# First A^T W products started matrix by matrix, and the last chunk worked in two token halves

## Chip, cores and metric

One core of one Trainium2 chip. The metric is the device time of one execution in microseconds, as the median of several. At this core count a run counts as slow when it lies more than 1.5% above the fastest of its kernel.

## The reference, cut to what matters

```python
# q, k, v: (4, 6144, 256); w1, w2, w3: (256, 768); w_out: (768, 256); fp32 in and out
qn = q / (norm(q, axis=1) + 1e-6)
kn = k / (norm(k, axis=1) + 1e-6)
s = kn.transpose(0, 2, 1) @ qn / tau             # 256 x 256 for each of 4 batches
a = softmax(s)                                   # rows sum to 1
x = (v @ a).reshape(24576, 256)
h = maximum(maximum(x @ w1, x @ w2), x @ w3)
out = h @ w_out
```

The kernel never builds `x`. It multiplies A^T into each W once per batch (`aw`), so that `h = max over m of v @ aw[m]`.

## The kernel before

PE is the matrix engine (PEld in the profile is its weight loads), ACT the scalar, DVE the vector and POOL the GpSimd engine; SP only sends transfers here. PSUM is the memory that PE writes its products to, and to evict is to copy them out of it. Work runs in 48 chunks of 512 tokens. PE forms three h products for each of six column blocks (`h_block`); ACT copies the first out of PSUM, and DVE takes two maxima with the other two. The output products of a chunk (`o_steps`) stand between the h blocks of the next. PSUM has six buffers for h and other products (`ps_h`) and two more (`ps_x`). The parts that the change touches:

```python
def rowsums(et):                       # 1/sum of the exponentials, by four tiny matmuls
    rs_ps = htile("rs_ps")
    ...PE.matmul(rs_ps[:, ic:ic + 1], lhsT=et[:, j, ic * P:(ic + 1) * P], rhs=ones_c, ...)
    DVE.reciprocal(out=rinv, in_=rs_ps[:, 0:CC])

def aw_part(et, rinv, aw, fp, w):      # 12 products, 6 evictions, ACT and DVE in turn
    for m in range(3):
        for ic in range(CC):
            ew = htile("ew_ps")
            for j in range(CC):
                PE.matmul(ew[:, :w], lhsT=et[:, j, ic * P:(ic + 1) * P], rhs=w_sb[m][:, j, fsl], ...)
            ...  # ACT.activation or DVE.tensor_scalar_mul into aw[m], times rinv

def v_transpose_pe(gi):                # 8 PE transposes of the first chunk's v, then
    ...
    ACT.activation(out=vt[:, :half, :], in_=ps[:, :half, :], func=AF.Copy)
    DVE.tensor_copy(out=vt[:, half:, :], in_=ps[:, half:, :])

def h_block(gi, aw, fc):
    for m in range(3):
        t = htile(f"h_ps{m}")
        for ic in range(CC):
            PE.matmul(t, lhsT=aw[m][:, ic, fsl], rhs=vt[:, :, ic, :], ...)   # 512 columns
        hp.append(t)
    ACT.activation(out=s_mx, in_=hp[0], func=AF.Copy)
    DVE.tensor_tensor(out=s_mx, in0=hp[1], in1=s_mx, op=ALU.max)
    DVE.tensor_tensor(out=ht[:, fc, :], in0=hp[2], in1=s_mx, op=ALU.max)

def o_last(gi):                        # the last chunk's output products, all at the end
    pss = [xtile("o_ps") for _ in range(TPC // 2)]
    ...  # 24 matmuls of 256 columns
    ACT.activation(out=o0, in_=pss[0], func=AF.Copy)      # 512 columns each
    DVE.tensor_copy(out=o1, in_=pss[1])
    ACT.dma_start(out=dst[:, 0:2, :], in_=o_sb[:, 0:2, :])
    SP.dma_start(out=dst[:, 2:4, :], in_=o_sb[:, 2:4, :])

ps = gram(0)
...  # 8 warm-up matmuls
et = softmax_t(*ps)
aw = alloc_aw()
rinv = rowsums(et)
v_transpose_pe(0)
aw_part(et, rinv, aw, 0, FT)
```

Of the kernel before, what the change touches and what calls it, by code (L numbers as in the profile page):

```python
# [10 lines left out]
FP32 = mybir.dt.float32  # L11
BF16 = mybir.dt.bfloat16
FP8 = mybir.dt.float8e4
AF = mybir.ActivationFunctionType
ALU = mybir.AluOpType
# [16 lines left out]
def kernel(  # L32
# [13 lines left out]
    PE = nc.tensor  # L46
    DVE = nc.vector
    ACT = nc.scalar
    POOL = nc.gpsimd
    SP = nc.sync  # L50

    B, N, C = q.shape
    d_ff = moe_w1.shape[1]
    d_model = C
    P = 128
    CC = C // P
    FC = d_ff // P
    CHUNK = 512
    TPC = CHUNK // P
    NG = N // P  # L60
    NCH = N // CHUNK
# [14 lines left out]
    sm = ctx.enter_context(tc.tile_pool(name="sm", bufs=2))  # L76
# [8 lines left out]
    def htile(name):  # L85
        return ps_h.tile([P, 512], FP32, tag="h", name=name)

    def xtile(name, cols=512, dtype=FP32):
        return ps_x.tile([P, cols], dtype, tag="x", name=name)
# [159 lines left out]
    def softmax_t(ps, rkb):  # L249
        n2q = sm.tile([P, CC], FP32, name="n2q")  # L250
        scr = sm.tile([P, P], FP32, name="scr")
        for j in range(CC):
            DVE.tensor_tensor_reduce(out=scr, in0=ps[j][:, C:C + P], in1=ident, scale=1.0, scalar=0.0,  # L253
                                     op0=ALU.mult, op1=ALU.add, accum_out=n2q[:, j:j + 1])
        lnq = sm.tile([P, CC], FP32, name="lnq")
        rq = sm.tile([P, CC], FP32, name="rq")
        ACT.activation(out=lnq, in_=n2q, func=AF.Ln)
        ACT.activation(out=rq, in_=lnq, func=AF.Exp, scale=-0.5, bias=neg_ln_tau)
        return exp_t([ps[j][:, 0:C] for j in range(CC)], rkb, rq)


    def alloc_aw():
        return [aw_pool.tile([P, CC, d_ff], BF16, name=f"aw{m}_sb", tag=f"aw{m}") for m in range(3)]

    def rowsums(et):
        rinv = sm.tile([P, CC], FP32, name="rinv")
# [3 lines that stand above are left out]
                PE.matmul(rs_ps[:, ic:ic + 1], lhsT=et[:, j, ic * P:(ic + 1) * P], rhs=ones_c,  # L270
                          start=(ic == 0 and j == 0), stop=(j == CC - 1), skip_group_check=True)
        DVE.reciprocal(out=rinv, in_=rs_ps[:, 0:CC])
        return rinv

    def aw_part(et, rinv, aw, fp, w):
        fsl = slice(fp * w, (fp + 1) * w)
        n = 0
# [4 lines that stand above are left out]
                    PE.matmul(ew[:, :w], lhsT=et[:, j, ic * P:(ic + 1) * P], rhs=w_sb[m][:, j, fsl],  # L282
                              start=(j == 0), stop=(j == CC - 1))
                if n % 2 == 0:
                    ACT.activation(out=aw[m][:, ic, fsl], in_=ew[:, :w], func=AF.Copy,  # L285
                                   scale=rinv[:, ic:ic + 1])
                else:
                    DVE.tensor_scalar_mul(out=aw[m][:, ic, fsl], in0=ew[:, :w],  # L288
                                          scalar1=rinv[:, ic:ic + 1])
                n += 1  # L290


    vts = {}
    hts = {}
# [12 lines left out]
    def v_transpose_pe(gi):  # L307
        v_sb = v_tiles.pop(gi).rearrange("p t c -> p (t c)")
        vt = vt_tile(gi)
        vt_ps = xtile("vt_ps", cols=TPC * C, dtype=BF16)  # L310
        for i in range(TPC * CC):
            PE.matmul(vt_ps[:, i * P:(i + 1) * P], lhsT=v_sb[:, i * P:(i + 1) * P], rhs=ident,
                      is_transpose=True, start=(i == 0), stop=(i == CC * TPC - 1))
        half = TPC * CC // 2
        ps = vt_ps.rearrange("p (i n) -> p i n", n=P)
        ACT.activation(out=vt[:, :half, :], in_=ps[:, :half, :], func=AF.Copy)
        DVE.tensor_copy(out=vt[:, half:, :], in_=ps[:, half:, :])

    def h_block(gi, aw, fc):
        vt = vts[gi]  # L320
        ht = hts[gi]
        fsl = slice(fc * P, (fc + 1) * P)
        hp = []
        for m in range(3):
            t = htile(f"h_ps{m}")
            for ic in range(CC):
                PE.matmul(t.rearrange("p (t n) -> p t n", t=TPC), lhsT=aw[m][:, ic, fsl], rhs=vt[:, :, ic, :], start=(ic == 0), stop=(ic == CC - 1))  # L327
            hp.append(t)
        s_mx = mx_pool.tile([P, CHUNK], BF16, name="s_mx")
        ACT.activation(out=s_mx, in_=hp[0], func=AF.Copy)  # L330
        DVE.tensor_tensor(out=s_mx, in0=hp[1], in1=s_mx, op=ALU.max)  # L331
        DVE.tensor_tensor(out=ht[:, fc, :], in0=hp[2], in1=s_mx, op=ALU.max)  # L332

    def o_steps(gi):

# [18 lines left out]

        return [lambda t=t: step(t) for t in range(TPC)]

    def o_last(gi):

        ht = hts[gi]
        o_sb = o_pool.tile([P, TPC, d_model], FP32, name="o_sb")  # L360
        pss = [xtile("o_ps") for _ in range(TPC // 2)]
        for fcs in (range(FC - 1), (FC - 1,)):
            for t in range(TPC):
                half = slice((t % 2) * d_model, (t % 2 + 1) * d_model)
                for fc in fcs:
                    PE.matmul(pss[t // 2][:, half], lhsT=ht[:, fc, t * P:(t + 1) * P], rhs=wo_sb[:, fc, :],  # L366
                              start=(fc == 0 and t % 2 == 0), stop=(fc == FC - 1), skip_group_check=True)
        dst = out_r[gi // NCH, gi % NCH]
        o0 = o_sb[:, 0:2, :].rearrange("p t d -> p (t d)")
        o1 = o_sb[:, 2:4, :].rearrange("p t d -> p (t d)")  # L370
        ACT.activation(out=o0, in_=pss[0], func=AF.Copy)
        DVE.tensor_copy(out=o1, in_=pss[1])  # L372
        ACT.dma_start(out=dst[:, 0:2, :], in_=o_sb[:, 0:2, :])
        SP.dma_start(out=dst[:, 2:4, :], in_=o_sb[:, 2:4, :])


    ps = gram(0)
    warm_ps = htile("warm_ps")
    for i in range(8):
        PE.matmul(warm_ps, lhsT=ident, rhs=warm, start=(i == 0), stop=(i == 7))  # L380
    et = softmax_t(*ps)
    aw = alloc_aw()
    rinv = rowsums(et)
    v_transpose_pe(0)
    aw_part(et, rinv, aw, 0, FT)
    v_transpose(1)

    guard = consts.tile([P, 1], BF16, name="guard")
# [10 lines left out]
    for b in range(B):  # L399
        more = b + 1 < B  # L400
        if more:
            alloc_qk(b + 1)
        for ch in range(NCH):
            gi = b * NCH + ch
            hts[gi] = ht_pool.tile([P, FC, CHUNK], BF16, name="ht_sb")
            load_v(gi + 4)
            v_transpose(gi + 2)
            if gi == 1:
                hold_loads(2)
            if more and 1 <= ch < 9:  # L410
                load_k(b + 1, (ch - 1) * 6, 6)
                load_q(b + 1, (ch - 1) * 6, 6)
            gaps = [[] for _ in range(FC)]
            if ch == 0:
                if b == 0:
                    for fp in range(1, d_ff // FT):
                        gaps[2 * fp - 2].append(lambda fp=fp: aw_part(et, rinv, aw, fp, FT))
                else:
                    gaps[0].append(lambda: aw_part(et, rinv, aw, 1, FH))
            for s, f in enumerate(pending):  # L420
                gaps[s + 1].append(f)
            if more and 3 <= ch < 11:
                g0 = (ch - 3) * 6
                for i, (which, g) in enumerate(((1, g0), (1, g0 + SQW), (0, g0), (0, g0 + SQW))):
                    gaps[(0, 2, 3, 5)[i]].append(lambda which=which, g=g: square_piece(b + 1, which, g))
            if more and ch == 10:
                gaps[5].append(lambda: fold(b + 1))
            if more and ch == NCH - 1:
                st = {}
                gaps[0].append(lambda: st.update(n=norms(b + 1)))  # L430
                gaps[1].append(lambda: st.update(e=exp_t(gs, *st["n"])))
                gaps[4].append(lambda: st.update(r=rowsums(st["e"])))
            for fc in range(FC):
                h_block(gi, aw, fc)
                for f in gaps[fc]:
                    f()
            pending = o_steps(gi)
            if more and ch == NCH - 2:
                gs = gram_kq(b + 1)
            if more and ch == NCH - 1:  # L440
                et, rinv = st["e"], st["r"]
                aw = alloc_aw()
                aw_part(et, rinv, aw, 0, FH)
    o_last(B * NCH - 1)
    keep_order(tc)


# [33 lines left out]
```

## Time and profile before

| | before |
|---|---|
| median of 3 runs | 576.62 us (576.47 to 576.75) |
| span of the profiled run | 574.9 us |
| PE / DVE / ACT busy | 97% / 71% / 53% |
| PE without a hole from | 39.78 us |
| last PE work, last eviction, span end | 570.43, 571.15, 574.9 us |

Lines of the chain of waits read "start us, length us, what" and are a path back from the last instruction; lines of the timeline read "start us, us, engine, line, operation, out<-in, count, [idle before <- what ended it]". The line numbers of the two kernels differ: h products are L327 before and L360 after, the second maximum L332 and L366.

### The profile page before, as it was taken

How to read it: one execution, taken by the hardware profiler on the slowest of the kernel's cores; microseconds unless marked ns; L12 is line 12 of the kernel's file. 1: busy time of each engine (PE TensorE's matmuls, PEld its weight loads, DVE VectorE, ACT ScalarE, POOL GpSimd, SP SyncE). 2: the span in 40 equal slices, each digit the busy share in tenths (PEclk: the TensorE clock that was granted, in tenths of full speed). 3: DMA queues.
4: the chain of work that ended last, by engine and by line, in shares of the span. 5: the costliest groups of instructions: out<-in, count | busy, mean ns of one | idle time of the engine just before them, and what ended most of it. 6: DMA issues, size and time to landing. Idle time of an engine off the chain costs nothing.

```text
span 574.9 us, 9325 instructions
## 1 busy us (share of the span) xinstructions
PE 555.1 (97%) x3328; PEld 328.5 (57%) x3328; DVE 406.4 (71%) x627; ACT 307.2 (53%) x530; POOL 227.3 (40%) x235
## 2 busy tenths in 40 slices
PE   3789999999999999999999999999999999999996
PEld 3655555555755555555575555555575555555554
DVE  0048777777577777777748777777848778778774
ACT  1034567677454466776735447767646444444442
POOL 4232257776731028777761006777760000000000
PEclk9999999999999999999999999999999999999999
DMA  9998998885598228977378526788535234322111
GB/s 142 107 144 157 130 178 124 157 133 113 102 118 164 59 66 155 133 152 130 75 131 130 114 75 101 157 131 130 125 84 127 66 82 129 74 91 76 56 73 74
DMA packets 75951, 65.62 MB, mean 114 GB/s; under 512 B 52353, under 2 KB 61953, under 8 KB 75905
## 3 DMA queue, kind: packets, MB, share of 16 engines
q0 software_dynamic: 18928, 26.48, 39.1%
q1 hardware_dynamic: 56832, 38.28, 22.9%
q8 instruction: 26, 0.43, 0.3%
q10 hardware_dynamic: 144, 0.26, 0.1%
q14 instruction: 21, 0.16, 0.1%
HBM read 78.64 MB, written 25.17 MB: 181 GB/s over the span
## 4 chain that ended last, share of the span: by engine, by line
PE 93%; DMA 5%; ACT 0%; DVE 0%; issue 0%; POOL 0%; DVEq 0%; POOLq 0%
PE h_ps L327 65%; PE o_ps L346 21%; DMA q_sb<-in_q_dram 4%; PE gram L235 3%; PE ew_ps L282 3%; DMA k_sb<-in_k_dram 2%; PE o_ps L366 0%; PE gram L178 0%; PE n_ps L216 0%; PE n_ps L218 0%; ACT et L246 0%; PE gram L180 0%; DVE o_sb L372 0%; POOL k_sb L99 0%; DVE scr L253 0%
## 5 line engine op out<-in xcount | busy, mean ns | idle before, releaser
L327 PE MATMUL h_ps<-vt_sb,aw_sb 128*128 128x512 bf16 x1728 | 406.6, 379 | 0.0
L331 DVE TENSOR_TENSOR s_mx<-h_ps,s_mx 128x512 bf16<-128x512 f32 x288 | 197.9, 687 | 98.1 <-ACT s_mx L330 97.1
L327 PEld LDWEIGHTS <-aw_sb 128*128 128x128 bf16 x1728 | 168.2, 98 | 163.0 <-DVE aw_sb L288 3.7
L330 ACT ACTIVATE s_mx<-h_ps 128x512 bf16<-128x512 f32 x288 | 171.4, 595 | 130.7 <-PE h_ps L327 130.7
L332 DVE TENSOR_TENSOR ht_sb<-h_ps,s_mx 128x512 bf16<-128x512 f32 x288 | 199.2, 692 | 30.7 <-PE o_ps L346 0.5
L204 POOL TENSOR_TENSOR acc<-acc,sq 128x768 f32<-128x768 f32 x90 | 147.7, 1651 | 70.7 <-ACT sq L198 70.5
L346 PE MATMUL o_ps<-wo_sb,ht_sb 128*128 128x256 bf16 x1128 | 153.9, 273 | 0.0
L346 PEld LDWEIGHTS <-ht_sb 128*128 128x128 bf16 x1128 | 110.4, 98 | 52.9
L349 ACT ACTIVATE o_sb<-o_ps 128x512 f32<-128x512 f32 x94 | 56.1, 597 | 83.1 <-PE o_ps L346 83.1
L110 POOL DMA_DIRECT2D v_sb<-in_v_dram x48 | 26.8, 562 | 88.5 <-DMA vt_sb<-v_sb 86.6
L198 ACT ACTIVATE sq<-q_sb 128x768 bf16<-128x768 fp8e4 x48 | 40.5, 844 | 0.0
L198 ACT ACTIVATE sq<-k_sb 128x768 bf16<-128x768 fp8e4 x48 | 40.1, 835 | 0.0
L201 POOL CAST acc<-sq 128x768 f32<-128x768 bf16 x6 | 4.9, 821 | 64.6 <-ACT sq L198 64.6
L102 POOL DMA_DIRECT2D q_sb<-in_q_dram x32 | 17.7, 555 | 10.7 <-DMA k_sb<-in_k_dram 9.7
L166 PE MATMUL kk<-k_sb 128*128 128x256 fp8e4 x48 | 7.8, 339 | 11.7 <-DVE k_sb L152 5.4
L285 ACT ACTIVATE aw_sb<-ew_ps,rinv 128x384 bf16<-128x384 f32 (+1 forms) x27 | 14.4, 546 | 5.7 <-PE ew_ps L282 4.8
L282 PE MATMUL ew_ps<-w_sb,et 128*128 128x384 bf16 (+1 forms) x108 | 17.1, 308 | 0.0
L235 PE MATMUL gram<-k_sb,q_sb 128*128 128x512 fp8e4 x144 | 16.8, 277 | 0.0
L99 POOL DMA_DIRECT2D k_sb<-in_k_dram x29 | 16.0, 554 | 1.0 <-POOLq L462 0.8
L235 PEld LDWEIGHTS <-q_sb 128*128 128x256 fp8e4 x144 | 15.9, 136 | 0.6
L178 PE MATMUL gram<-k_sb,q_sb 128*128 128x512 fp8e4 x48 | 10.7, 323 | 3.4 <-DMA q_sb<-in_q_dram 3.4
L166 PEld LDWEIGHTS <-k_sb 128*128 128x256 fp8e4 x48 | 6.5, 182 | 12.8 <-DMA k_sb<-in_k_dram 6.3
(52 smaller groups left out, 103.6 us busy)
## 6 DMA issues: line engine op xcount, KB each, us to landing
out_dram<-o_sb SPq DMA_DIRECT2D x47, 512.0 KB, 2.8
v_sb<-in_v_dram POOLq DMA_DIRECT2D x48, 256.0 KB, 3.7
k_sb<-in_k_dram POOLq DMA_DIRECT2D x24, 192.0 KB, 5.3
q_sb<-in_q_dram POOLq DMA_DIRECT2D x24, 192.0 KB, 6.8
k_sb<-in_k_dram POOLq DMA_DIRECT2D x5, 256.0 KB, 10.8
q_sb<-in_q_dram POOLq DMA_DIRECT2D x5, 256.0 KB, 19.4
w_sb<-in_moe_w_dram POOLq DMA_DIRECT2D x9, 128.0 KB, 5.7
kf<-in_k_dram SPq DMA_DIRECT2D x2, 512.0 KB, 4.3
```

The costliest lines, as they stand in the source:

```text
L102: POOL.dma_start(out=qk[b][0][:, g0:g0 + w, :], in_=q_r[b][:, g0:g0 + w, :])
L110: POOL.dma_start(out=t, in_=v_r[gi // NCH, gi % NCH])
L198: ACT.activation(out=sq, in_=src, func=AF.Square)
L204: POOL.tensor_tensor(out=acc, in0=acc, in1=sq, op=ALU.add)
L235: PE.matmul(g[:, j * C:(j + 1) * C], lhsT=qt[:, tsl, j * P:(j + 1) * P], rhs=kt[:, tsl, :], start=(tp == 0 and j == 0), stop=(tp == NG // ...
L282: PE.matmul(ew[:, :w], lhsT=et[:, j, ic * P:(ic + 1) * P], rhs=w_sb[m][:, j, fsl], start=(j == 0), stop=(j == CC - 1))
L327: PE.matmul(t.rearrange("p (t n) -> p t n", t=TPC), lhsT=aw[m][:, ic, fsl], rhs=vt[:, :, ic, :], start=(ic == 0), stop=(ic == CC - 1))
L330: ACT.activation(out=s_mx, in_=hp[0], func=AF.Copy)
L331: DVE.tensor_tensor(out=s_mx, in0=hp[1], in1=s_mx, op=ALU.max)
L332: DVE.tensor_tensor(out=ht[:, fc, :], in0=hp[2], in1=s_mx, op=ALU.max)
L346: PE.matmul(st["ps"][:, half], lhsT=ht[:, fc, t * P:(t + 1) * P], rhs=wo_sb[:, fc, :], start=(fc == 0), stop=(fc == FC - 1))
L349: ACT.activation(out=st["o"][:, t - 1:t + 1, :].rearrange("p t d -> p (t d)"), in_=st["ps"], func=AF.Copy)
```

## The change

Its intent: in the head, fill PE's wait for the exponentials with the transposes and with the products whose weights have landed, and let DVE copy v first; in the tail, have half of the last chunk's output evicted and sent before the end. Cut to its core:

```diff
+    def aw_first(et, aw):
+        ...
+        products(0, (0, 1))          # first half of et, matrices 0 and 1
+        sums(0)
+        sums(1)
+        DVE.reciprocal(out=rinv, in_=rs_ps[:, 0:CC])
+        products(1, (0, 1))
+        for j in range(CC):
+            products(j, (2,))
+        ...                          # the same six evictions
@@ v_transpose_pe
+        DVE.tensor_copy(out=vt[:, half:, :], in_=ps[:, half:, :])
         ACT.activation(out=vt[:, :half, :], in_=ps[:, :half, :], func=AF.Copy)
-        DVE.tensor_copy(out=vt[:, half:, :], in_=ps[:, half:, :])
@@ h_block takes a token slice, so its matmuls, copy and maxima can be 256 columns wide
-    def o_last(gi):
+    def last_chunk(gi, aw, pending):
+        ...
+        for fc in range(FC):
+            h_block(gi, aw, fc, slice(0, HT))
+            if 1 <= fc <= len(pending):
+                pending[fc - 1]()             # output products of the chunk before
+        for fc in range(FC):
+            h_block(gi, aw, fc, slice(HT, TPC))
+            if fc >= FC - HT:
+                first_half(fc - (FC - HT))    # 6 output products; the 2nd call evicts and sends
+        ...                                   # 12 products of the second half, in two banks
+        ACT.activation(out=o_sb[:, HT, :], in_=pss[0][:, 0:d_model], func=AF.Copy)
+        DVE.tensor_copy(out=o_sb[:, HT + 1, :], in_=pss[1][:, 0:d_model])
+        ACT.dma_start(out=dst[:, HT, :], in_=o_sb[:, HT, :])
+        SP.dma_start(out=dst[:, HT + 1, :], in_=o_sb[:, HT + 1, :])
@@ head
-    for i in range(8):               # warm-up matmuls
+    for i in range(6):
     et = softmax_t(*ps)
+    v_transpose_pe(0)
     aw = alloc_aw()
-    rinv = rowsums(et)
-    v_transpose_pe(0)
-    aw_part(et, rinv, aw, 0, FT)
+    rinv = aw_first(et, aw)
```

More of the change, by code (lines that the diff above doesn't have):

```diff
@@ L290, in aw_part, with sums, products @@
                 n += 1
+    def aw_first(et, aw):
+        rinv = sm.tile([P, CC], FP32, name="rinv")
+        rs_ps = xtile("rs_ps")
+        parts = [(m, ic, htile("ew_ps")) for m in range(3) for ic in range(CC)]
+        def sums(j):
+            for ic in range(CC):
+                PE.matmul(rs_ps[:, ic:ic + 1], lhsT=et[:, j, ic * P:(ic + 1) * P], rhs=ones_c,
+                          start=(ic == 0 and j == 0), stop=(j == CC - 1), skip_group_check=True)
+        def products(j, ms):
+            for m, ic, ew in parts:
+                if m in ms:
+                    PE.matmul(ew[:, :FT], lhsT=et[:, j, ic * P:(ic + 1) * P], rhs=w_sb[m][:, j, 0:FT],
+                              start=(j == 0), stop=(j == CC - 1))
+        products(0, (0, 1))
[5 more added lines that the diff above has]
+            products(j, (2,))
+        for n, (m, ic, ew) in enumerate(parts):
+            if n % 2 == 0:
+                ACT.activation(out=aw[m][:, ic, 0:FT], in_=ew[:, :FT], func=AF.Copy, scale=rinv[:, ic:ic + 1])
+            else:
+                DVE.tensor_scalar_mul(out=aw[m][:, ic, 0:FT], in0=ew[:, :FT], scalar1=rinv[:, ic:ic + 1])
+        return rinv
     vts = {}
@@ L315, in v_transpose_pe, with h_block @@
         ps = vt_ps.rearrange("p (i n) -> p i n", n=P)
+        DVE.tensor_copy(out=vt[:, half:, :], in_=ps[:, half:, :])
         ACT.activation(out=vt[:, :half, :], in_=ps[:, :half, :], func=AF.Copy)
-        DVE.tensor_copy(out=vt[:, half:, :], in_=ps[:, half:, :])
-    def h_block(gi, aw, fc):
+    def h_block(gi, aw, fc, tsl=slice(0, TPC)):
         vt = vts[gi]
-        ht = hts[gi]
+        n = (tsl.stop - tsl.start) * P
+        ht = hts[gi][:, fc, tsl.start * P:tsl.stop * P]
         fsl = slice(fc * P, (fc + 1) * P)
@@ L324, in h_block @@
         for m in range(3):
-            t = htile(f"h_ps{m}")
+            t = htile(f"h_ps{m}")[:, :n]
             for ic in range(CC):
-                PE.matmul(t.rearrange("p (t n) -> p t n", t=TPC), lhsT=aw[m][:, ic, fsl], rhs=vt[:, :, ic, :], start=(ic == 0), stop=(ic == CC - 1))
+                PE.matmul(t.rearrange("p (t n) -> p t n", n=P), lhsT=aw[m][:, ic, fsl], rhs=vt[:, tsl, ic, :],
+                          start=(ic == 0), stop=(ic == CC - 1))
             hp.append(t)
-        s_mx = mx_pool.tile([P, CHUNK], BF16, name="s_mx")
+        s_mx = mx_pool.tile([P, CHUNK], BF16, name="s_mx")[:, :n]
         ACT.activation(out=s_mx, in_=hp[0], func=AF.Copy)
         DVE.tensor_tensor(out=s_mx, in0=hp[1], in1=s_mx, op=ALU.max)
-        DVE.tensor_tensor(out=ht[:, fc, :], in0=hp[2], in1=s_mx, op=ALU.max)
+        DVE.tensor_tensor(out=ht, in0=hp[2], in1=s_mx, op=ALU.max)
     def o_steps(gi):
@@ L355, in o_steps, with products, first_half @@
         return [lambda t=t: step(t) for t in range(TPC)]
-    def o_last(gi):
-        ht = hts[gi]
+    def last_chunk(gi, aw, pending):
+        hts[gi] = ht_pool.tile([P, FC, CHUNK], BF16, name="ht_sb")
         o_sb = o_pool.tile([P, TPC, d_model], FP32, name="o_sb")
-        pss = [xtile("o_ps") for _ in range(TPC // 2)]
-        for fcs in (range(FC - 1), (FC - 1,)):
-            for t in range(TPC):
-                half = slice((t % 2) * d_model, (t % 2 + 1) * d_model)
-                for fc in fcs:
-                    PE.matmul(pss[t // 2][:, half], lhsT=ht[:, fc, t * P:(t + 1) * P], rhs=wo_sb[:, fc, :],
-                              start=(fc == 0 and t % 2 == 0), stop=(fc == FC - 1), skip_group_check=True)
-        dst = out_r[gi // NCH, gi % NCH]
-        o0 = o_sb[:, 0:2, :].rearrange("p t d -> p (t d)")
-        o1 = o_sb[:, 2:4, :].rearrange("p t d -> p (t d)")
-        ACT.activation(out=o0, in_=pss[0], func=AF.Copy)
-        DVE.tensor_copy(out=o1, in_=pss[1])
-        ACT.dma_start(out=dst[:, 0:2, :], in_=o_sb[:, 0:2, :])
-        SP.dma_start(out=dst[:, 2:4, :], in_=o_sb[:, 2:4, :])
+        dst = out_r[gi // NCH, gi % NCH]
+        HT = TPC // 2
+        def products(ps, t0, i, fcs):
+            c0 = i * d_model if t0 == 0 else 0
+            for fc in fcs:
+                PE.matmul(ps[:, c0:c0 + d_model], lhsT=hts[gi][:, fc, (t0 + i) * P:(t0 + i + 1) * P],
+                          rhs=wo_sb[:, fc, :], start=(fc == 0 and c0 == 0), stop=(fc == FC - 1),
+                          skip_group_check=True)
+        first = {}
+        def first_half(i):
+            if i == 0:
+                first["ps"] = xtile("o_ps")
+            products(first["ps"], 0, i, range(FC))
+            if i == HT - 1:
+                ACT.activation(out=o_sb[:, 0:HT, :].rearrange("p t d -> p (t d)"), in_=first["ps"], func=AF.Copy)
+                SP.dma_start(out=dst[:, 0:HT, :], in_=o_sb[:, 0:HT, :])
+        for fc in range(FC):
[6 more added lines that the diff above has]
+                first_half(fc - (FC - HT))
+        pss = [htile("o_ps") for _ in range(HT)]
+        for fcs in (range(FC - 1), (FC - 1,)):
+            for i in range(HT):
+                products(pss[i], HT, i, fcs)
+        ACT.activation(out=o_sb[:, HT, :], in_=pss[0][:, 0:d_model], func=AF.Copy)
+        DVE.tensor_copy(out=o_sb[:, HT + 1, :], in_=pss[1][:, 0:d_model])
+        ACT.dma_start(out=dst[:, HT, :], in_=o_sb[:, HT, :])
+        SP.dma_start(out=dst[:, HT + 1, :], in_=o_sb[:, HT + 1, :])
@@ L377 @@
     ps = gram(0)
     warm_ps = htile("warm_ps")
-    for i in range(8):
-        PE.matmul(warm_ps, lhsT=ident, rhs=warm, start=(i == 0), stop=(i == 7))
+    for i in range(6):
+        PE.matmul(warm_ps, lhsT=ident, rhs=warm, start=(i == 0), stop=(i == 5))
     et = softmax_t(*ps)
+    v_transpose_pe(0)
     aw = alloc_aw()
-    rinv = rowsums(et)
-    v_transpose_pe(0)
-    aw_part(et, rinv, aw, 0, FT)
+    rinv = aw_first(et, aw)
     v_transpose(1)
@@ L404 @@
             gi = b * NCH + ch
+            if gi == B * NCH - 1:
+                last_chunk(gi, aw, pending)
+                break
             hts[gi] = ht_pool.tile([P, FC, CHUNK], BF16, name="ht_sb")
@@ L443 @@
                 aw_part(et, rinv, aw, 0, FH)
-    o_last(B * NCH - 1)
     keep_order(tc)
```

## The prediction

> **What bounds the kernel now.** I read the page's busy shares first, then the chain that ended last, then the same chain cut to the head and to the tail, then the timeline of those two stretches and the landings of the early transfers.
>
> ```profile
> PE 555.1 (97%) x3328; PEld 328.5 (57%) x3328; DVE 406.4 (71%) x627; ACT 307.2 (53%) x530; POOL 227.3 (40%) x235
> ...
> PE 93%; DMA 5%; ACT 0%; DVE 0%; issue 0%; POOL 0%; DVEq 0%; POOLq 0%
> ```
>
> PE sets the end over 93% of the span; the 5% DMA is the first q and k, up to 31.3 us. So work saved off PE is worth nothing, and a microsecond that PE stands still in the head or works alone in the tail is worth a microsecond. The change touches only these two places. The head, as the chain gives it (start, length, what):
>
> ```profile
> 35.33 0.92 ACT et L246 x2
> 36.24 0.05 issue
> 36.29 0.23 PE rs_ps L270 x3
> 36.52 0.47 PE vt_ps L312 x8
> 36.98 1.31 PE ew_ps L282 x12
> 38.30 0.22 PE h_ps L327
> 38.51 0.01 issue
> 38.52 1.25 PE h_ps L327 x5
> 39.78 1.31 PE ew_ps L282 x12
> ```
>
> PE waits for both halves of the exponentials (et), then does row sums, transposes of v, the first 12 products A^T W, and the first h block. From 39.78 on the chain is PE without a hole. The waits inside this stretch, from the timeline:
>
> ```profile
> 35.88 0.10 PEld L270 LDWEIGHTS <-et 128*128 128x128 bf16 x1 [0.43 <-ACT et L246]
> 36.28 0.14 PEld L270 LDWEIGHTS <-et 128*128 128x128 bf16 x3 [0.30 <-ACT et L246]
> 37.65 0.42 DVE L317 COPY vt_sb<-vt_ps 128x512 bf16<-128x512 bf16 x1 [0.93 <-ACT vt_sb L316]
> ```
>
> The reader is to see that PE is empty for most of 35.9 to 36.3, between the two et halves, while 20 matmuls that could run there stand behind the row sums; and that DVE's copy waits for ACT's, which puts its three evictions at 37.99 to 39.25 in the way of the first h block (1.47 us for six matmuls that take 1.30 elsewhere). The weights of the first products were issued at 23.34, 25.80 and 28.25 and landed after
>
> ```profile
> w_sb<-in_moe_w_dram POOLq DMA_DIRECT2D x1, 128.0 KB, 12.0
> ...
> w_sb<-in_moe_w_dram POOLq DMA_DIRECT2D x1, 128.0 KB, 10.2
> ...
> w_sb<-in_moe_w_dram POOLq DMA_DIRECT2D x1, 128.0 KB, 8.4
> ```
>
> that is at 35.3, 36.0 and 36.65, so the third matrix is the last that an earlier start could meet. The tail:
>
> ```profile
> 556.11 3.88 PE h_ps L327 x18
> ...
> 567.80 2.63 PE o_ps L366 x24
> 570.43 0.02 issue
> 570.46 0.69 DVE o_sb L372
> ...
> out_dram<-o_sb ACTq DMA_DIRECT2D x1, 256.0 KB, 2.0
> out_dram<-o_sb SPq DMA_DIRECT2D x1, 256.0 KB, 2.4
> ```
>
> 24 output products, one DVE eviction of 512 columns, and the slower of two stores: issued at 571.17, landed 573.6, span end 574.9.
>
> **What the Trainium skill says.** "TensorE: Matmul & The Clock Gate", section Back-to-back issue gap: N/2.4 + 2.5 ns when warm, so 216 ns at 512 columns and 109 at 256. The trace agrees: 3.88/18 = 0.2156, and 0.66/6 = 0.109 for the 256-column output products. Halving a matmul costs only about 1 ns in each half. "VectorE: DVE Perf Modes", section on the TRN2 errata: an fp32 tensor_tensor takes (N+151)/0.96 ns, 691 at 512 and 424 at 256: halving it does not halve it. The trace has 687 and 692 ns for the two maxima at 512, and 416 for a 256-column tensor_tensor out of PSUM (e_in). "PSUM — Partial Sum Buffer", section PSUM bank collisions raise a hardware error: two engines may not touch one bank at once, so a dependency is put between them; the DVE copy's 0.93 us wait for ACT's copy of the same bank shows it. "DMA: Bandwidth & Descriptors", section Anatomy of one DMA: a fixed part plus bytes over 436 GB/s. The last stores move at about 419 GB/s at their peak, so 128 KB is 0.31 us.
>
> **The change, head.** Two of eight warm-up matmuls go: 34.05 + 6 x 0.216 puts their end at 35.35 in place of 35.8; both lie inside the wait for et. The eight transposes move ahead of it. They need v (landed 34.7) and a bank that the first e_in product leaves at about 35.2, so they run 35.35 to 35.82: 0.47 off the path. At 35.88 (first et half) start four products of the first two matrices, 4 x 0.109 = 0.44, to 36.32, just when the second half arrives (36.28); the second matrix at 36.10 meets its landing at 36.0. Four row sums, 4 x 0.077 = 0.3: 36.62. Eight more products, 0.87: 37.49; those of the third matrix start at 37.05, 0.4 after its landing. Evictions: DVE copies its half of v at 35.9 to 36.3, ACT after it to 36.93, then both evict aw from about 36.9, three each at 0.42 apart, done at 38.2. The h block needs its first weights at 37.4 and its last at about 38.4, so it runs unstalled: 37.49 + 1.29 = 38.78 against 39.78. The later weight parts (landed 37.4 to 38.7, then 39.3 to 40.8) stay ahead of use. Head: -1.0 us, carried to the end because PE has no hole after it.
>
> **The change, tail.** PE's work is the same but for 72 h matmuls at 0.109 against 36 at 0.2156: +0.07. The last eviction falls from 691 to about 424 ns (256 columns): -0.27. The last stores are 2 x 128 KB in place of 2 x 256 KB, the other 256 KB having been sent about 1.1 us before: at 419 GB/s some 0.6 us less moves after the last eviction, of which I take -0.5, because runs of 1 KB per partition may be a little slower.
>
> **What it adds: DVE becomes the bound in the halves.** At 512 columns DVE needs 1.39 us per h block (maxima start at 558.06, 558.67, 559.46: 0.61 and 0.79 apart); PE needs 1.29, and two blocks of buffers cover 0.1. At 256 columns I take 0.27 off each spacing: 0.34 + 0.52 = 0.86 of DVE against 0.654 of PE. Six h buffers are two blocks, so the third product of a block waits for the second maximum of the block two before. With ACT at 0.38 for a half block, that maximum ends some 1.69 us after its own block's start, and PE wants the buffer at 1.308 + 0.436 = 1.74: no slack to begin with. Output products (0.654 for six) after half blocks 1 to 4 of the first half give DVE time. Between the last block of the first half and the fifth of the second there are none. Stepping it through: the second half's third, fourth and fifth blocks each wait 0.2, then six output products and the sixth block run free. That is +0.6. At the entry of the chunk, the second half block needs the buffer of the full block before it, whose second maximum ends 2.64 after that block's start, where PE would want it at 1.29 + 0.654 + 0.436 = 2.38: +0.3. Stalls +0.9. At the very end the last maximum, 1.7 after its half block's start, is covered by the 6 + 10 matmuls that stand before the last two.
>
> Sum: -1.0 + 0.07 + 0.9 - 0.27 - 0.5 = -0.8. 576.62 - 0.8 = 575.8 us.
>
> **Rivals.** (a) No stall in the halves: if the buffers are given back sooner than I step it, the tail gives its full 0.7 and the kernel loses 1.7: 574.9. For it: the 30 h matmuls without fillers at 45.06 take 6.54 us, hardly a stall, though DVE lags there as well. Against it: there the slack at the start is 0.8 us, here it is nil. (b) DVE worse than 0.86, or the stall reaching the first output products: the tail loses 1.5 and the kernel stays at 576.4 to 577. (c) The head's gain turns into a wait for the weights: the second matrix lands within 0.1 us of its use, and semaphore delay could make it late; that takes 0.1 to 0.2 of the 1.0, not more, because the et halves bound the same place. A wait for the third has 0.4 of margin. (d) The head's gain is given back at the second chunk, whose v (landed 42.0) and transpose are not moved: but it is needed only at about 50.6, so I give this little.
>
> **Range and chances.** The head is sure to about 0.2, the stalls to 0.5, stores and eviction to 0.2, and runs of the same kernel here span 0.3. So 574.8 to 576.8. Two per cent is 11.5 us, more than all that the change touches; only a slow state or a mistake in the trace's reading could give it: within 2% 0.98.
>
> **What would show it.** After: row sums behind four products, the second weight part starting near 38.8; then every chunk 1.0 earlier, at the last chunk still 1.0. In the last chunk, h stretches of PE with means above 0.109 per matmul at the places named, PE waits on DVE's second maximum, DVE near full from the first half's end, DVE maxima near 420 ns. Last eviction near 0.42 us, last landing under 2 us after issue. Wrong would be: no PE hole in the last chunk (then rival a), or the head's 1.0 missing at chunk two (c, d).

## The result, and the profile after

The changed kernel took 575.94 us (median of 6; its four fast runs 575.86 to 575.98) against 576.72 of the kernel before (6 runs), 0.78 us less. The ratio of the fast runs is 0.9987, 95% interval 0.9972 to 1.0002: the same, by the 2% measure, and an interval that just holds no difference. So that the change gains at all rests on fast runs that do not overlap (575.86 to 575.98 against 576.47 to 576.75) and on the trace. A ratio here is the mean time of one kernel's fast runs over that of the other's of the same rounds, so it is not quite the ratio of the medians. Two of the six runs were slow, 586.05 and 591.13; I come back to them at the end of the experiments.

The chain in the head of the changed kernel:

```profile
34.23 1.24 PE warm_ps L436 x5
35.47 0.45 PE vt_ps L343 x8
35.92 0.62 PE ew_ps L306 x4
36.53 0.08 PE rs_ps L300 x4
36.61 0.90 PE ew_ps L306 x8
37.51 1.41 PE h_ps L360 x6
38.92 1.31 PE ew_ps L282 x12
```

The transposes have moved ahead of 35.9, four products stand in front of the row sums, and the second weight part starts at 38.92 in place of 39.78: 0.86 us earlier. In the timeline DVE no longer waits for ACT to copy v:

```profile
35.95 0.42 DVE L347 COPY vt_sb<-vt_ps 128x512 bf16<-128x512 bf16 x1 [0.51 <-PE vt_ps L343]
...
36.41 0.60 ACT L348 ACTIVATE vt_sb<-vt_ps 128x512 bf16<-128x512 bf16 x1 [0.22 <-DVE vt_sb L347]
...
37.44 0.12 PEld L360 LDWEIGHTS <-aw_sb 128*128 128x128 bf16 x2 [0.21 <-ACT aw_sb L318]
```

The third line is the cost that stayed: the first h block's weights cannot be loaded before ACT's first eviction.

The 0.86 us hold until the last chunk: the 18 h matmuls that began at 556.11 before begin at 555.26 after. From there the chain of the changed kernel reads:

```profile
562.45 2.34 PE h_ps L360 x20
564.79 0.43 DVE ht_sb L366
...
565.26 0.81 PE h_ps L360 x6
...
566.11 0.84 PE h_ps L360 x6
...
570.26 0.43 DVE o_sb L428
```

Now DVE stands in a chain that was PE alone. 36 h matmuls and their waits fill 562.45 to 566.95, 4.50 us; at the 0.109 us of the halves elsewhere they take 3.93, so 0.57 us is waiting. PE ends at 570.24, only 0.19 us before the kernel before did. DVE's pace in this stretch, from the timeline of DVE alone:

```profile
564.26 0.41 DVE L365 TENSOR_TENSOR s_mx<-h_ps,s_mx 128x256 bf16<-128x256 f32 x1
564.78 0.42 DVE L366 TENSOR_TENSOR ht_sb<-h_ps,s_mx 128x256 bf16<-128x256 f32 x1
565.12 0.41 DVE L365 TENSOR_TENSOR s_mx<-h_ps,s_mx 128x256 bf16<-128x256 f32 x1
```

And the last two stores, from the view of DMA issues (KB, us from issue to landing):

```profile
out_dram<-o_sb ACTq DMA_DIRECT2D x1, 128.0 KB, 1.9
out_dram<-o_sb SPq DMA_DIRECT2D x1, 128.0 KB, 2.1
```

The maxima start 0.52 and 0.34 us apart, 0.86 for a half block, against 0.654 of PE. The last eviction is 0.43 us in place of 0.69, and the last store lands 2.1 us after issue in place of 2.4.

### The profile page after: what moved, and what is told of

Its sections match the earlier page's. It is cut to its first block, busy times and chain, and to the rows that moved or that the text cites. A ratio compares the mean times of both kernels' runs of the same rounds, so it can differ in the third digit from the quotient of the medians.

```text
span 574.1 us, 9430 instructions
## 1 busy us (share of the span) xinstructions
PE 555.2 (97%) x3361; PEld 331.9 (58%) x3362; DVE 407.6 (71%) x639; ACT 308.6 (54%) x537; POOL 227.3 (40%) x235
## 4 chain that ended last, share of the span: by engine, by line
PE 94%; DMA 5%; issue 0%; DVE 0%; POOL 0%; POOLq 0%
PE h_ps L360 65%; PE o_ps L380 21%; DMA q_sb<-in_q_dram 3%; PE gram L235 3%; PE ew_ps L282 2%; DMA k_sb<-in_k_dram 2%; PE o_ps L401 0%; PE gram L178 0%; PE ew_ps L306 0%; PE n_ps L216 0%; PE warm_ps L436 0%; PE n_ps L218 0%; PE gram L180 0%; POOL k_sb L99 0%; PE vt_ps L343 0%
## 5 line engine op out<-in xcount | busy, mean ns | idle before, releaser
L360 PE MATMUL h_ps<-vt_sb,aw_sb 128*128 128x512 bf16 (+1 forms) x1764 | 407.2, 375 | 0.1
L365 DVE TENSOR_TENSOR s_mx<-h_ps,s_mx 128x512 bf16<-128x512 f32 (+1 forms) x294 | 198.8, 676 | 97.6 <-ACT s_mx L364 96.5
L360 PEld LDWEIGHTS <-aw_sb 128*128 128x128 bf16 x1764 | 171.8, 98 | 161.0 <-DVE aw_sb L288 2.8
L364 ACT ACTIVATE s_mx<-h_ps 128x512 bf16<-128x512 f32 (+1 forms) x294 | 172.3, 586 | 131.4 <-PE h_ps L360 130.0
L366 DVE TENSOR_TENSOR ht_sb<-h_ps,s_mx 128x512 bf16<-128x512 f32 (+1 forms) x294 | 200.2, 681 | 31.4 <-PE o_ps L380 0.5
L285 ACT ACTIVATE aw_sb<-ew_ps,rinv 128x384 bf16<-128x384 f32 (+1 forms) x24 | 13.2, 555 | 5.7 <-PE ew_ps L282 4.8
L282 PE MATMUL ew_ps<-w_sb,et 128*128 128x384 bf16 (+1 forms) x96 | 15.6, 313 | 0.0
## 6 DMA issues: line engine op xcount, KB each, us to landing
q_sb<-in_q_dram POOLq DMA_DIRECT2D x5, 256.0 KB, 19.4
```

Of the source, the lines that this page charges most:

```text
L360: PE.matmul(t.rearrange("p (t n) -> p t n", n=P), lhsT=aw[m][:, ic, fsl], rhs=vt[:, tsl, ic, :], start=(ic == 0), stop=(ic == CC - 1))
L366: DVE.tensor_tensor(out=ht, in0=hp[2], in1=s_mx, op=ALU.max)
```

## The experiments

Each kernel was run with the kernel before on the same chip. My theory: the head is worth 0.86 us; the tail's smaller eviction and stores are worth about 0.6, and the token halves give that back, because at 256 columns DVE is slower than PE and returns the PSUM buffers late. The times below are the medians of the fast runs; on the chips of these runs the kernel before took 576.71 to 576.74. By the 2% measure every one of these kernels is the same as before. The 95% interval lies wholly under 1 only for the two spread kernels, the wide ones with the new head, and one maximum; for the others it holds no difference, and what is said of them rests on the medians and on the traces. (Holds keep loads back for a while; they are explained under the slow runs.)

| kernel | fast runs, us | against before | slow runs |
|---|---|---|---|
| the change | 575.90 | -0.8 | 2 of 6 |
| head only | 575.88 | -0.9 | 2 of 6 |
| tail only | 576.55 | -0.2 | 0 of 5 |
| output products spread out | 575.33 | -1.4 | 1 of 5 |
| wide last chunk, early first store | 575.34 | -1.4 | 1 of 5 |
| one maximum (wrong result) | 575.48 | -1.2 | 1 of 4 |
| eight warm-ups | 576.26 | -0.5 | 0 of 4 |
| ACT copies v first | 576.19 | -0.5 | 0 of 4 |
| one weight matrix (wrong result) | 575.96 | -0.8 | 1 of 6 |
| the change again | 576.01 | -0.7 | 4 of 8 |
| wide last chunk, head as before | 576.15 | -0.6 | 0 of 6 |
| wide last chunk and holds | 575.48 | -1.3 | 0 of 6 |
| spread out and holds | 575.37 | -1.4 | 0 of 6 |

### The two parts alone

Head only: the last chunk as in the kernel before (`o_last` back, `last_chunk` gone).

> Head of the change (six warm-ups, transposes first, products of the first two matrices before the row sums, DVE's v copy first), last chunk as before. My theory (the two parts do not touch each other, each is worth what its own stretch of the chain shows): the head is worth what the second weight part gained in the trace, 39.62 to 38.76, so -0.86 us against before, 575.8. Rival (the head's gain is given back later, and the whole gain of the change is the tail's): within 0.2 us of before.

Measured 575.88, 0.86 under the kernel before on that chip (ratio's interval 0.9975 to 1.0003). By the medians the head's gain is whole and nothing gives it back.

Tail only: `aw_first`, the order of the copies and the six warm-ups undone.

> Last chunk of the change, head as before. My theory: PE pays 0.66 us in the last chunk (0.07 for narrower matmuls, about 0.57 of waits for buffers that DVE gives back late) and the last eviction and store get 0.61 us shorter, so within 0.15 us of before. Rival (the tail is a gain by itself and the head gives something back): -0.5 us or more.

Measured 576.55, 0.19 under before, a little past the 0.15 I had allowed; its ratio's interval, 0.9981 to 1.0006, holds no difference at all. The same waits stand in its chain:

```profile
563.13 2.34 PE h_ps L360 x20
```

So the two parts add up roughly (-0.86 and -0.19 against -0.82 for both; in the profiles the same old head starts the second weight part at 39.60 here and at 39.78 before, so 0.2 is within what runs differ by), and the tail by itself is close to nothing. The rival, a tail that gains half a microsecond, falls.

### What the tail pays: order of the same work

```diff
         for fc in range(FC):
             h_block(gi, aw, fc, slice(0, HT))
-            if 1 <= fc <= len(pending):
-                pending[fc - 1]()
+            if fc % 2 == 1:
+                pending[fc // 2]()
         for fc in range(FC):
             h_block(gi, aw, fc, slice(HT, TPC))
-            if fc >= FC - HT:
-                first_half(fc - (FC - HT))
+            if fc == 1:
+                pending[3]()
+            elif fc % 2 == 1:
+                first_half(fc // 2 - 1)
```

> The change, with the six groups of output products (four of the chunk before, two of the first half) put after every second half block (1, 3, 5 of each half) in place of 1 to 4 and then 4, 5. Same instructions, same matmul widths, same work for each engine. My theory (DVE at 0.86 us a half block against 0.65 of PE, buffers run out where no output products stand between): PE's waits vanish, -0.5 to -0.6 us against the changed kernel, 575.35. Rival (256-column matmuls, each with its own weight load, cost PE the 0.6 us themselves): no change, 575.9.

Measured 575.33, ratio 0.9972 (0.9960 to 0.9985). The chain in the same stretch:

```profile
562.47 1.31 PE h_ps L360 x12
563.78 0.66 PE o_ps L380 x6
```

1.31/12 is 0.109: no wait is left, with the same instructions, widths and weight loads. What cost 0.57 us was where the output products stood, not the narrow matmuls. Two half blocks and six output products are 1.97 us of PE, and DVE needs 1.72 for the two blocks.

### Half of DVE's work (wrong result on purpose)

```diff
-        DVE.tensor_tensor(out=s_mx, in0=hp[1], in1=s_mx, op=ALU.max)
+        if tsl.start == 0:
+            DVE.tensor_tensor(out=s_mx, in0=hp[1], in1=s_mx, op=ALU.max)
```

> The change with the first of the two DVE maxima left out in the second token half of the last chunk (wrong result on purpose: the second product is not used there). PE's work stays. My theory (DVE rate sets when buffers come back): DVE needs 0.4 a half block, under PE's 0.65, and PE's waits of 0.57 us vanish; 575.35, and PE's h matmuls in that stretch are 0.109 apart. Rival (ACT's copy, or the matmuls themselves, hold PE up): 575.9 still.

```profile
562.26 3.93 PE h_ps L360 x36
```

36 matmuls without a hole, with the output products where the change has them. Measured 575.48 (three fast runs, 575.09 to 575.54), relative error 0.058 as it must be. So the narrow matmuls alone do not make the wait, and without this work of DVE there is none. Spread and this run are two ways to the same end, one by giving DVE time and one by taking work from it.

ACT is not cleared by this. The run also takes away the only reader of the second product, so its buffer is free at once, and by the semaphores the later products get other buffers than in the change. And in the change's own trace ACT has a part (lines from the timelines of ACT and of DVE):

```profile
562.48 0.60 ACT L383 ACTIVATE o_sb<-o_ps 128x512 f32<-128x512 f32 x1 [0.71 <-PE o_ps L380]
...
563.39 0.42 DVE L365 TENSOR_TENSOR s_mx<-h_ps,s_mx 128x256 bf16<-128x256 f32 x1 [0.62 <-ACT s_mx L364]
...
565.67 0.38 ACT L364 ACTIVATE s_mx<-h_ps 128x256 bf16<-128x256 f32 x1 [0.48 <-PE h_ps L360]
```

ACT evicts outputs before it copies the last block of the first half, so DVE stands idle for 0.62 us just before its run of maxima. And by the semaphores in the trace the first two of PE's three waits (0.15 and 0.21 us) end with DVE's second maximum, but the third ends with ACT's copy of the block just before (565.67 to 566.06; 0.20 us), with 0.03 more for DVE's first maximum. No run takes ACT's part alone away, so how the 0.57 us divides between DVE and ACT is not shown.

### The tail's gain without token halves

The last chunk's h blocks stay 512 wide. Token tiles 0 and 1 share a bank, tiles 2 and 3 have one each, and only the order of the 24 output products changes:

```diff
+        for t, fcs in ((0, range(5)), (1, range(5)), (2, range(4)), (0, (5,)), (1, (5,))):
+            products(t, fcs)
+        ...  # ACT evicts tiles 0 and 1, SP sends them
+        products(2, (4, 5))
+        products(3, range(FC))
+        ...  # ACT and DVE evict 256 columns each and send 128 KB each
```

> Head of the change; the last chunk's h blocks 512 columns wide as before, and only the output products ordered so that the first two token tiles end 8 products before the end and are evicted and sent then; the last two tiles are evicted at 256 columns and sent as 128 KB each. My theory (the tail's gain comes from the smaller last eviction and store alone, token halves only add DVE work): the head's 0.86 and the tail's 0.61 both kept, nothing paid: 576.7 - 1.45 = 575.25. Rival (halves are needed for the tail's gain, as only then the first store is out of the way): 575.6 or more.

Measured 575.34, ratio 0.9972 (0.9960 to 0.9985).

```profile
566.91 2.69 PE o_ps L407 x24
...
569.62 0.42 DVE o_sb L417
```

The 24 products take 2.69 us, 0.06 more than before, and the small eviction and stores are kept. With the head as before:

> Head as before, last chunk 512 columns wide with the output products ordered for an early first store (as in the run with both). My theory (the parts add up, the tail's gain is the smaller last eviction and stores alone): 0.55 to 0.61 us under before, 576.15, and no slow run. Rival (the tail's gain needs token halves): within 0.2 of before.

Measured 576.15, 0.58 under before. The gain of the tail never needed the halves. Whether it needs the first two tiles to be out of the way was not run: both wide kernels send them early.

### The head, taken apart

Eight warm-ups again:

> The change with eight warm-up matmuls in place of six. My theory (the warm-ups end at 35.5 in the changed kernel, just as the transposes can start, so two more push the transposes, and with them the first products, 0.43 us later; the second weight matrix is then no longer waited for, which gives back 0.1): +0.3 us against the changed kernel, 576.25. Rival (warm-ups hide behind the wait for the exponentials): no change. Beside that: of the kernels with the new head 6 of 22 runs so far were slow ones, of those with the old head none of 22; if the two missing warm-ups are what lets them in, none of these is slow; if it is the order of the head, one or two are.

Measured 576.26, 0.36 above the change.

```profile
34.12 1.67 PE warm_ps L436 x7
35.80 0.45 PE vt_ps L343 x8
```

1.67 us of warm-up in place of 1.24, and the transposes follow at once. In the changed order the warm-ups are no longer hidden: each stands in front of the transposes.

The copies of v in the old order:

> The change with the two copies of the transposed v back in the old order (ACT's half before DVE's). My theory (DVE's copy then waits for ACT's, which waits for ACT's second exponential until 36.2; DVE's reciprocal of the row sums stands behind its copy and comes at 37.2 in place of 36.65, and all six evictions wait for it): the first h block starts 0.4 to 0.5 us later, 576.35. Rival (the evictions are late anyway because of the products): within 0.1 of the changed kernel.

Measured 576.19, 0.29 above the change; I had expected 0.45. The chain goes as I said, but the reciprocal began at 37.06 and not 37.2 (the chain counts it from the end of DVE's copy):

```profile
36.20 0.49 ACT vt_sb L347
...
36.72 0.42 DVE vt_sb L348
37.14 0.09 DVE rinv L312
```

So the two swapped lines are worth about a third of the head's gain.

All first products from one weight matrix (wrong result: `w_sb[0]` for `w_sb[m]`):

> The change with the first A^T W products all taken from the first weight matrix (wrong result on purpose), so that none waits for the second and third to land. My theory (in the changed kernel the third product started at 36.16, when the second matrix landed, 0.1 later than PE could): the four products take 0.44 in place of 0.53 to 0.62 and the kernel gains 0.1 us, 575.8. Rival (the row sums, which need the second half of the exponentials at 36.3, would wait in any case): the wait moves there and nothing is gained.

Not settled by its time: 575.96 (fast runs 575.82 to 577.53), not to be told from the change. Its profile, a slow run but the same as the others up to 40 us, has the first four products in 0.53 us, not in 0.44. Most other kernels with this head have 0.53 or 0.54 too; in three profiles (the change, the change again, one maximum) the third product waited for the second matrix to land, in the change's until 36.16, and they took 0.61 or 0.62. So the wait for the second matrix is 0 to 0.09 us, from run to run, and my 0.44 left out something else. With eight warm-ups, where the exponentials are there before the transposes end, they did take 0.44: the other 0.09 is the first product's wait for the first half of the exponentials.

### Slow runs, counted and left open

> The changed kernel itself once more, on one chip with the next two and the kernel before. Theory and rival expect 575.9 in its fast runs. It is run to count slow executions: of kernels whose first h block starts at 37.3 to 37.6 us, 8 of 33 so far took 586 us or more; of those where it starts at 37.7 or later, none of 34. If the early start is what lets them in, one or two of these are slow and none of before; if they come at random, as many of before.

Four of its eight listed runs took 585.03 to 602.93 us; its fast ones 575.95 to 577.67, median 576.01. Counted over all runs without the holds below, kernels in which the first h block starts at 37.3 to 37.7 us had 12 slow runs of 40, and those in which it starts later (before, tail only, wide with the old head, eight warm-ups, ACT first) none of 48. The start is that of each kernel's one profile, and the line between the groups was moved after the counts: this run's 37.68 was put with the early ones, and the next is 37.76. (The note above has 8 of 33 and none of 34 for what were 8 of 32 and none of 31.) The profile of one slow run, that of the one-matrix kernel, has PE waiting for the transposes of v that DMA makes:

```profile
PE h_ps L360 <- DMA vt_sb<-v_sb: 8.3, 3, 3.7
```

That is of its waits from 60 to 170 us (total, times, longest). Two transposes stand in its chain:

```profile
68.93 24.57 DMA vt_sb<-v_sb
...
126.38 25.63 DMA vt_sb<-v_sb
```

The other slow profile, that of the change again, has two as well, 22.57 us from 69.01 and 25.09 us from 112.38.

In fast profiles of the change the transpose sent at 68.8 lands after 11.2 us, in the kernel before after 10.9, both behind a burst of eight loads at 57 to 61 us (the one sent at 58.4 takes 19.4), and most later ones after about 3.4. In the two slow profiles all those sent from 69 to 136 us take 15 to 26 us, long after that burst, so the burst alone does not account for them. "DMA: Bandwidth & Descriptors" in the Trainium skill, section Issuing engines are not separate DMA queues, says that DMAs of all queues run on the same 16 engines and interleave; the transposes of SP's queue behind the loads of POOL's agree with it. Two more holds break the burst up:

```diff
-            if gi == 1:
-                hold_loads(2)
+            if 1 <= gi <= 3:
+                hold_loads(gi + 1)
```

> Head of the change and the wide last chunk with ordered outputs, and two more holds: the k and q pieces of chunks 2 and 3 are not sent until the transposes of chunks 3 and 4 have landed. Theory on the slow runs (in the slow profile the v transpose sent at 68.9 took 24.6 us and PE waited 3.7 us for it at 93; in fast profiles of the changed kernel it takes 11.2, of the kernel before 10.9, both behind a burst of eight loads at 57 to 61 us; the earlier PE meets the end of that burst): with the burst broken up the v transposes of chunks 4 and 5 land in under 10 us, fast runs stay at 575.3 and none of five is slow. Rival (the holds starve the squares of batch 1, or the transposes are slow for another reason): 576 or more, or a slow run still.

Measured 575.48, ratio 0.9982 (0.9967 to 0.9996); that transpose landed after 7.5 us.

> The change with output products after every second half block, and the two more holds of the k and q pieces. Theory: the two gains are independent, fast runs at 575.4 (spread alone 575.34; the holds cost at most 0.1, as the wide chunk showed, 575.37 and 575.48), the v transpose of chunk 5 lands in about 7.5 us instead of 11.2, and no run at 585 us or more; of the kernels with the early start and no holds 12 of 40 listed runs were that slow, with the holds none of 6 so far, of those with the later start none of 48. (An earlier note of mine, 8 of 33 and none of 34, miscounted: 8 of 32 and none of 31.) Rival (the holds do nothing for the slow runs and the six were luck): one or two slow runs.

Measured 575.37, ratio 0.9974 (0.9954 to 0.9995), the transpose after 7.6 us. No slow run in the twelve of both; at 12 of 40 that would happen by chance once in about 72 times (0.7 to the 12th power, an estimate from the counts). The estimate takes the runs as independent. Single runs near 577 us are left in these two kernels, and near 578 in the kernel before. That slow runs go with the early start, and went away with the holds, are counts, and the cause stays open; that the earlier PE meets the end of the burst is only argued.

## Why the prediction was right

The sum was right (575.8 predicted, 575.94 measured; -0.8 against -0.78), and so were most of the places of gain and loss. Three of its terms were off, by 0.14, -0.33 and 0.16; that these cancel is luck.

- **Head, -1.0 predicted, -0.86 measured.** Order as told. (The prediction's "20 matmuls that could run there" is too many: its own working, and the change, put 12 before the row sums, eight transposes and four products.) The four products took 0.62 where 0.44 was reckoned, the row sums 0.08 where 0.3, and the six h matmuls 1.41 where 1.29, because their weights wait for the first eviction. Rival (c), the wait for the second matrix, is real and small: 0 to 0.09.
- **Narrower matmuls, +0.07.** Borne out by the spread kernel, 0.109 each.
- **Waits for DVE, +0.9 predicted, 0.57 measured.** DVE's pace was right to the hundredth, 0.86 a half block, and the waits are at the third to fifth blocks of the second half: 0.15, 0.21 and 0.23 us beyond the spacing of the starts, where 0.2 each was told. The 0.3 at the chunk's entry did not come: PE runs from 555.26 through 18 matmuls in 2.60 us, which is six at 0.2156 and twelve at 0.109. The step that failed is that six buffers come back in turn, so that the third product of a block waits for the second maximum of the block two before. The compiled program takes buffers in another order: by the semaphores in the trace, at the entry that product waits for ACT and not for DVE, and is not held up; in the second half the first products of the third and fourth blocks wait for the second maximum of the block three before, and the first product of the fifth for ACT's copy of the block just before. Which buffer it is cannot be read off the pool's size. So the waits came where they were told, but not wholly by the path that was told, and that 0.2 each came so close is in part luck.
- **Eviction, -0.27 predicted, -0.26 measured. Stores, -0.5 predicted, -0.34 measured**: from the end of the last eviction to the end of the span 3.75 us before (574.9 - 571.15) and 3.41 after (574.1 - 570.69). The prediction took the eviction's 424 ns from a formula that the page gives for an fp32 tensor_tensor, measured there at 512 and 2048 columns: it is an estimate, and for a copy; the copy took 0.43 us. Half the bytes did not take off what 419 GB/s would give, and the last store landed 2.1 us after issue where under 2 was told; why is not shown.

The sum of the measured: -0.86 + 0.07 + 0.57 - 0.26 - 0.34 = -0.82, against 0.8 between the spans. Rival (a), no stall, is what the spread kernel built: it predicted 574.9 for that and 575.33 was measured: the head and the stores gave 0.3 less than told, and the kernel before took 0.1 more. Rivals (b) and (d) did not come in fast runs; in the slow ones PE did wait for transposes of v, several chunks later than (d) has it.

## What to carry to other kernels

When work is cut narrower, reckon the period of every engine at the new width before believing the overlap: fixed costs do not halve (DVE's maximum took 0.69 us at 512 columns and 0.42 at 256), and an engine that was only just behind at 512 (1.39 us of DVE against 1.29 of PE, covered by two blocks of buffers) can hold PE up at 256 (0.86 against 0.654). Putting other work of PE, here output products, evenly between the narrow blocks made -0.8 into -1.4 with the same instructions. And look for a way to the same end that leaves the width alone: ordering 24 products did as much as the token halves.

## What the Trainium skill lacked or had wrong

- "DMA: Bandwidth & Descriptors", section Anatomy of one DMA, gives its fit of 2.0 us plus bytes over 436 GB/s for the path from GpSimd; for stores issued from SP and ACT the page has a first-byte latency but no fit. (The prediction's use of the 436 GB/s for such stores went beyond the section.) Here 512 KB landed 2.6 us after issue, 256 KB after 2.0 (2.0 and 2.4 for two at once) and 128 KB after 1.9 and 2.1 (two at once); the fit gives 3.2, 2.6 and 2.3.
- The same page, section DMA Transpose (X-bar), gives no landing time, in quiet or under load. Here a transpose of 256 KB landed after about 3.4 us in quiet, 19.4 and then 11.2 behind a burst of eight loads (the second 7.5 with the burst broken up), and up to 25.6 in a slow run.
- "VectorE: DVE Perf Modes" has the durations right (0.41 to 0.42 us at 256 columns, with one operand fp32 in PSUM and one bf16, where its formula for fp32 gives 0.424, an estimate at that width). But no page gives a figure for the spacing of a dependent pair, which set the pace: 0.52 us to the maximum that needs the one before, 0.34 to the one that does not.
- "TensorE: Matmul & The Clock Gate", section Back-to-back issue gap, gives N/2.4 + 2.5 ns, which the prediction used, for an isolated matmul only, and says that a stream of weight loads and matmuls runs at about 131 ns a matmul at 512 columns. Here every h matmul has its own weight load (1728 of each in the kernel before) and the stream runs at 0.2156 us, 0.109 at 256 columns: the formula holds for the stream too, and the 131 does not show here.
